# The feed-forward gradient at the normalised h1 as seven block products per pair of token tiles

## The chip, the cores and the metric

The kernel runs on one core of a Trainium2 chip. The metric is the device time of one execution in microseconds (us); lower is better. A core has TensorE (matrix products, PE in the profile), VectorE (DVE), ScalarE (ACT), GpSimd (POOL) and SyncE (SP). Each takes its own instructions in order; SP, POOL and ACT also issue DMAs. Products are accumulated in PSUM, here four tiles of two banks.

## The reference

Forward and backward of one block, S = 2048 tokens, width 640, 32 heads of 20, inner width 1728, bf16:

```
h   = x + ((phi(q) kv) / den) @ wo         q, k, v = LN(x) @ wqkv
      phi(t) = where(t > 0, t + 1, exp(t)) + 1e-6
      kv = sum_s phi(k) v    z = sum_s phi(k)    den = phi(q).z + 1e-6
out = h + (silu(LN(h) @ w_gate) * (LN(h) @ w_up)) @ w_down
```

Returned are out and the gradients of x, wqkv, wo, w_gate, w_up and w_down for a given gradient of out. What the change is about is the gradient at the normalised h1 (h before its layer norm is divided out): `dhn = [dg du] @ [w_gate w_up]^T`, a product of 2048 x 3456 by 3456 x 640, and what follows it: the layer norm's backward pass gives dh1, `dp = dh1 @ W2^T`, then dq, and dz, the gradient of z.

## The kernel before, in words

Tokens are 16 tiles of 128. The kernel first computes q and k, then the attention part (h1, its normalised form `hn`, its reciprocal deviation `rstd2`), then the FFN in four groups of inner columns (448, 448, 448, 384): gate and up products (L731, L736), elementwise work that makes the gradients `dd` (L764), and a `dw_group` for the weight gradients, whose products it already forms as seven block products (L646) beside plain ones (L806). `dd` is transposed by DMA and stored to `scr_dT` in HBM, 27 blocks of 128 rows for each token tile; the transposed weights stand in `wgT` (14 and 13 blocks of 128 x 640).

After the FFN comes the stage of this document (L846 to L921). In its loop over t:

- `load_cols` (L165) brings two token tiles of `scr_dT` (1728 KB) into one of four `strips` buffers.
- `mm_row` (L104) makes ps_dhn: 27 products for each of two column halves.
- `ln_bwd` (L141): ScalarE scales ps_dhn by rstd2 and sums it, VectorE multiplies with hn and sums, ScalarE makes `a`, VectorE adds twice; dh1 is transposed by DMA on SP's queue.
- Three tiles later (`LAG_C`): ps_dp from the transposed dh1; then VectorE: multiply by phi(q), sum per head, nS1 = -S1/den, zb x nS1, add, clamp phi(q) to phi'(q), two multiplications to dq. phi(q) is read from `scr_pq` by a POOL DMA; `pqs_tm` (phi(q)/den) is made from it (L886).
- `dz_add` (L833): two fp32 operations a tile, ten in the loop, six later under ps_dwqk.

`gt_part` (L858) sums over all tokens the products of dh1 and pqs_tm into five ps_gt; three of them start before the last ps_dp. Then ps_dwqk, ps_dkvt, ps_wk2, ps_dk and ps_dxn follow (L966 to L1077).

The framework gives buffers from pools (`big`: 5, `strips`: 4, `fpool`: 6, `psum`: 4) and makes an instruction wait for a free one. Within `tc.manual_schedule(engines=...)` the named engines keep the written order; elsewhere a planner orders instructions. In the stage before, SP and POOL keep the written order and TensorE, VectorE and ScalarE are planned.

Of the kernel before, what the change touches and what calls it, by code (L numbers as in the profile page):

```python
# [8 lines left out]
FP32 = mybir.dt.float32  # L9
# [6 lines left out]
P = 128  # L16
# [4 lines left out]
def kernel(  # L21
# [24 lines left out]
    MTA = 5  # L46
    assert (S, D, F) == (2048, 640, 1728)
# [35 lines left out]
    scr_pq, scr_pq_v = dram_tm("scr_pq", D)  # L83
    scr_h1, scr_h1_v = dram_tm("scr_h1", D)
# [527 lines left out]
    fpool = wB.enter_context(tc.tile_pool(name="fpool", bufs=6))  # L612
    zpad = wB.enter_context(tc.tile_pool(name="zpool", bufs=1)).tile([P, 4, 64], BF16, name="zpad")
    nc.gpsimd.memset(zpad[:], 0.0)

    with tc.manual_schedule(engines={EngineType.SP}):
# [6 lines left out]
        def hn_blk(m, k, u):  # L623
            i = 2 * m + u
            return hn[:, 8 * k:8 * k + 8, i * P:(i + 1) * P]

        def dw_group(g, w, m_s, dd, dw, dwd_part, dgu_part):
# [28 lines left out]
            S3 = [sums.tile([P, 8, P], BF16, name="S3", tag="S3", bufs=2) for _ in U]  # L656
            dw([dwd_part(0), dwd_part(1)], nc.vector.tensor_copy, first=True)
            for u in U:
                tt(S[u][:], hn_blk(1, 0, u), hn_blk(1, 1, u), ALU.add)
            for u in U:  # L660
                tt(S3[u][:], hn_blk(0, 0, u), hn_blk(1, 0, u))
            dw([dgu_part(4, 0), dgu_part(4, 1)], copy)
# [12 lines left out]
            store(ev, 0, 0)  # L675
            dw([dwd_part(4)], nc.vector.tensor_copy)
# [4 lines left out]
            tt(T3, B22, B12)  # L681
            dw([dwd_part(2), dwd_part(3)], nc.vector.tensor_copy)
# [4 lines left out]
            for u in U:  # L687
                prod(pa[u][:, 0, :w], S3[u], T3, False)
                copy(out=u3[:, u, :], in_=pa[u][:, 0, :w])
                tt(S[u][:], hn_blk(0, 1, u), S[u][:])  # L690
            ev = fw("dwev")
            tt(ev[:, :, :w], pc[:, :, :w], u3, ALU.add)
            store(ev, 1, 1)
            late = m_s[:, 12:16, :].rearrange("p (k u) n -> p k u n", k=2)
# [27 lines left out]
        for g in range(4):  # L722
# [53 lines left out]
            if g == 0:  # L776
                wdT = strips.tile([P, DT, 2 * GM], BF16, name="wdT", tag="S")
                load_wdT(wdT, 2)
            elif g == 1:
                wgT[0] = big.tile([P, 14, D], BF16, name="wgT", tag="B")  # L780
                for gg in range(2):
                    tr_wgT(gg)
                    load_wgu(gg + 2)
            elif g == 2:
                dm_t[3] = strips.tile([P, ST, GM], BF16, name="dm3", tag="S")
                act_load(dm_t[3][:, :, :GW[3]], scr_dm_v)
                wgT[1] = big.tile([P, 13, D], BF16, name="wgT", tag="B")
                tr_wgT(2)
                tr_wgT(3)
            else:  # L790
                for c in range(4):
                    pool_store(scr_m_v[:, c * 4:(c + 1) * 4, F:FT * P], m_s[:, c * 4:(c + 1) * 4, w - 64:w])
                pool_store(mat_v(scr_dwdT)[:, 0:4, F:FT * P], zpad[:])
                pool_store(mat_v(scr_dwdT)[:, 4, F:FT * P], zpad[:, 0, :])
                load_cols(0, act_load)

# [33 lines left out]
    mats = M.tile([P, 3 * DT * D], BF16, name="mats", tag="M")  # L830
    zacc = M.tile([P, D], FP32, name="zacc", tag="Z")

    def dz_add(t, tmp):  # L833
        prod = tmp if t else zacc[:]
        nc.vector.tensor_tensor(out=hb(prod), in0=hb(pqs_tm[:, t, :]), in1=bc(nS1[:, t, :]), op=ALU.mult)
        if t:
            nc.vector.tensor_tensor(out=zacc[:], in0=zacc[:], in1=tmp, op=ALU.add)
# [8 lines left out]
    with tc.manual_schedule(engines={EngineType.SP, EngineType.Pool}):  # L846
        W2T = mat(0, DT, D)
        nc.sync.dma_start(out=W2T[:], in_=mat_v(scr_W2T))
        woT = mat(DT * D, DT, D)
        dh1 = dh2  # L850
        pqs_tm = big.tile([P, ST, D], BF16, name="pqs_tm", tag="B")
        pqr = {}
        dwds = {}
        dh1Ts = {}

        gts = {}

        def gt_part(ps, i, t0, t1):  # L858
            for ci, (n0, n1) in enumerate(NCH):
                for t in range(t0, t1):  # L860
                    nc.tensor.matmul(ps[:, ci, :320], lhsT=dh1[:, t, i * P:(i + 1) * P], rhs=pqs_tm[:, t, n0:n1],  # L861
                                     start=(t == 0), stop=(t == ST - 1))

        ZL = 10
        ztmp = mats[:, 11 * D:13 * D].bitcast(FP32)
        dq = [strips.tile([P, 8, D], BF16, name="dq", tag="S") for _ in range(2)]
        for t in range(ST + LAG_C):
            if t < ST:
                if t % 2 == 0 and 2 < t + 2 < ST:
                    load_cols(t // 2 + 1)  # L870
                cols = colp[t // 2]
                if t >= 2:
                    dwds[t - 2] = wk("dwd", pool=1)
                    nc.sync.dma_start_transpose(out=dwds[t - 2][:].unsqueeze(1), in_=scr_dwdT[:, (t - 2) * P:(t - 1) * P])
                ps = mm("ps_dhn")
                mm_row(ps, lambda k: cols[:, t % 2, k, :],
                       lambda k, n0, n1: wgT[k // 14][:, k % 14, n0:n1], NKT)
                ln_bwd(ps, hn[:, t, :], rstd2[:, t:t + 1], dh2[:, t, :], dh1[:, t, :], 0)
                dh1T = wk("dh1T", pool=1)
                dh1Ts[t] = dh1T[:].rearrange("p (k c) -> p k c", c=P)  # L880
                last_dh1T = nc.sync.dma_start_transpose(out=dh1Ts[t], in_=dh1[:, t, :]).ins
            u = t - LAG_C + 1
            if u in range(ST):
                pqr[u] = wk("pqr", pool=1)
                nc.gpsimd.dma_start(out=pqr[u][:], in_=scr_pq_v[:, u, :])
                nc.vector.tensor_tensor(out=hb(pqs_tm[:, u, :]), in0=hb(pqr[u][:]), in1=bc(rall[:, u, :]), op=ALU.mult)  # L886
            if 0 <= t - LAG_C - 1 < ZL:
                dz_add(t - LAG_C - 1, ztmp)
            if 3 <= t < FT + 3:
                dwd = dwds.pop(t - 3)  # L890
                r0 = (t - 3) * P
                nc.gpsimd.dma_start(out=out_6[r0:min(r0 + P, F), :], in_=dwd[:min(P, F - r0), :])
            if t % 2 == 1 and t < 2 * DT:
                tr_piece(woT, A_wo, t // 2)
            if t % 4 == 2 and t >= 6:

                nc.gpsimd.dma_start(out=hn[:, t - 6:t - 2, :], in_=x_v[:, t - 6:t - 2, :])
            u = t - LAG_C
            if u < 0:
                continue  # L900
            if u == ST - 1:
                for i in range(3):
                    gts[i] = mm("ps_gt")
                    gt_part(gts[i], i, 0, ST - 3)
            pq = pqr.pop(u)
            dh1Tv = dh1Ts.pop(u)
            dp = wk("dp")
            ps = mm("ps_dp")
            mm_row(ps, lambda i: dh1Tv[:, i, :], lambda i, n0, n1: W2T[:, i, n0:n1], DT)
            nc.scalar.copy(out=half(dp[:]), in_=row(ps))  # L910
            pr = wk("pr")
            nc.vector.tensor_tensor(out=pr[:], in0=dp[:], in1=pq[:], op=ALU.mult)
            S1 = small.tile([P, H], FP32, name="S1", tag="S1", bufs=3)
            nc.vector.tensor_reduce(out=S1[:], in_=hb(pr[:]), axis=AX.X, op=ALU.add)
            nc.vector.scalar_tensor_tensor(out=nS1[:, u, :], in0=S1[:], scalar=-1.0, in1=rall[:, u, :],
                                           op0=ALU.mult, op1=ALU.mult)
            nc.vector.tensor_tensor(out=hb(pr[:]), in0=hb(zb[:]), in1=bc(nS1[:, u, :]), op=ALU.mult)
            nc.vector.tensor_tensor(out=dp[:], in0=dp[:], in1=pr[:], op=ALU.add)
            nc.vector.tensor_scalar(out=pq[:], in0=pq[:], scalar1=-1e-6, scalar2=1.0, op0=ALU.add, op1=ALU.min)
            nc.vector.tensor_tensor(out=dp[:], in0=dp[:], in1=pq[:], op=ALU.mult)  # L920
            nc.vector.tensor_tensor(out=hb(dq[u // 8][:, u % 8, :]), in0=hb(dp[:]), in1=bc(rall[:, u, :]), op=ALU.mult)  # L921

    with tc.manual_schedule(engines={EngineType.SP, EngineType.DVE}):
# [27 lines left out]
        for i in range(DT):  # L951
# [4 lines left out]
            else:  # L956
                gt_part(ps, i, ST - 3, ST)
            nc.scalar.copy(out=half(GT[:, i, :]), in_=row(ps))

# [44 lines left out]
        ztmp = ring[:, 0:2].rearrange("p a k c -> p (a k c)").bitcast(FP32)  # L1004
        for t in range(ZL, ZL + 2):
            dz_add(t, ztmp)
        dwqk(0, 0)
        kv_blocks(dKVT, "ps_dkvt", lambda i, a, b: woT[:, i, a:b], lambda i, a, b: GT[:, i, a:b])
        for t in range(ZL + 2, ST):
            dz_add(t, ztmp)  # L1010
        dzs = [wk("dzs"), wk("dzl")]
        nc.vector.tensor_copy(out=dzs[0][:], in_=zacc[:])
        nc.vector.tensor_tensor(out=dzs[1][:], in0=zacc[:], in1=dzs[0][:], op=ALU.subtract)
# [310 lines left out]
```

## Time and profile before

| | |
|---|---|
| time, median of 3 runs | 796.45 us (796.36 to 796.95) |
| the profiled execution | 796.25 us, span 794.5 us, granted clock 1.0 |
| TensorE busy | 790.2 us |
| VectorE busy | 566.9 us |
| first ps_dhn to end of ps_gt | 437.2 to 598.1 us |

A group's row gives line, engine, operation, output <- inputs, partitions x elements, count, then busy time and mean ns of one, then the idle time before it and who ended it. A matmul's duration overlaps that of the next, so its pace is read from the chain or the time line. Landing is the time from a DMA's issue to the arrival of its data.

### The profile page before, as it was taken

Reading aid. Unit: us, or ns where it says so; the run is one execution under the profiler, and the core shown is the slowest. Engines: PE = TensorE matmul, PEld = TensorE weight load, DVE = VectorE, ACT = ScalarE, POOL = GpSimd, SP = SyncE. Lnnn points to the kernel's source line nnn. Section 1 sums busy time; section 2 is a strip of 40 time slices with the busy share of each in tenths; the row PEclk is TensorE's granted clock in tenths of the full one; section 3 lists DMA queues with packets and bytes.
Section 4 is the critical chain, followed back from the end, with each engine's and each line's share of the span. In section 5 each row is a group of like instructions: output and inputs, shape, how many; then the busy total and the mean of one; then the engine's idle time right before and its main releaser. Section 6 shows DMA issues by size and latency. Waiting matters only on the chain.

```text
span 794.5 us, 13629 instructions
## 1 busy us (share of the span) xinstructions
PE 790.2 (99%) x5315; PEld 506.5 (64%) x5315; DVE 566.9 (71%) x1015; ACT 288.1 (36%) x414; POOL 172.7 (22%) x305
## 2 busy tenths in 40 slices
PE   9999999999999999999999999999999999999998
PEld 7776566555555555555666777777777777777665
DVE  7989988894497648845975259998897366635773
ACT  6962532760283045402831123223313133324010
POOL 4600047411201110012042102111221121113230
PEclk9999999999999999999999999999999999999999
DMA  9799999999679877892798657976598959999992
GB/s 259 161 241 305 198 225 254 257 264 234 176 160 236 211 175 191 217 246 68 147 216 217 247 152 193 211 197 168 127 238 177 177 135 155 189 223 261 208 259 83
DMA packets 286705, 160.11 MB, mean 202 GB/s; under 512 B 241564, under 2 KB 275485, under 8 KB 286640
## 3 DMA queue, kind: packets, MB, share of 16 engines
q1 hardware_dynamic: 268912, 99.56, 61.7%
q0 software_dynamic: 14832, 54.36, 22.4%
q10 hardware_dynamic: 2896, 5.33, 2.0%
q8 instruction: 41, 0.67, 0.4%
q14 instruction: 24, 0.20, 0.1%
HBM read 47.68 MB, written 53.66 MB: 128 GB/s over the span
## 4 chain that ended last, share of the span: by engine, by line
PE 97%; DMA 1%; DVE 1%; POOL 0%; issue 0%; SPq 0%; DVEq 0%
PE ps_dhn L108 15%; PE ps_dw L806 10%; PE ps_dxn L1069 8%; PE pu L736 7%; PE ps_wa L646 7%; PE pg L731 7%; PE ps_dwqk L986 5%; PE ps_dm L417 5%; PE ps_kq L305 4%; PE ps_oa L1139 4%; PE ps_wc L646 3%; PE ps_gt L861 3%; PE ps_dp L108 3%; PE ps_dk L108 3%; PE ps_y L508 3%; PE ps_a L571 3%
## 5 line engine op out<-in xcount | busy, mean ns | idle before, releaser
L108 PE MATMUL ps_dhn<-wgT,cols 128*128 128x320 bf16 x864 | 119.5, 299 | 0.0
L108 PEld LDWEIGHTS <-cols 128*128 128x128 bf16 x864 | 84.5, 98 | 32.9
L146 DVE CUSTOM_DVE_ANT_0 lb_a<-lb_dy,hn 128x640 bf16<-128x640 bf16 x32 | 26.4, 825 | 59.0 <-ACT lb_dy L144 59.0
L736 PE MATMUL pu<-wgu,hnT 128*128 128x448 bf16 (+1 forms) x320 | 63.6, 346 | 0.0
L731 PE MATMUL pg<-wgu,hnT 128*128 128x448 bf16 (+1 forms) x320 | 63.6, 346 | 0.0
L806 PE MATMUL ps_dw<-m_s,dh 128*128 128x448 bf16 (+1 forms) x320 | 60.4, 346 | 0.0
L1069 PEld LDWEIGHTS <-ring 128*128 128x128 bf16 x480 | 47.0, 98 | 18.2
L1069 PE MATMUL ps_dxn<-wqkvT,ring 128*128 128x320 bf16 x320 | 51.3, 299 | 0.0
L736 PEld LDWEIGHTS <-hnT 128*128 128x128 bf16 x320 | 31.3, 98 | 27.1
L806 PEld LDWEIGHTS <-dh 128*128 128x128 bf16 x320 | 31.3, 98 | 27.1
L731 PEld LDWEIGHTS <-hnT 128*128 128x128 bf16 x320 | 31.3, 98 | 27.0
L417 PEld LDWEIGHTS <-dh2T 128*128 128x128 bf16 x320 | 31.0, 98 | 25.1
L417 PE MATMUL ps_dm<-wdT,dh2T 128*128 128x448 bf16 (+1 forms) x240 | 46.5, 344 | 0.0
L144 ACT ACTIVATE lb_dy<-ps_dhn,rstd 128x640 bf16<-128x640 f32 x16 | 12.7, 794 | 91.5 <-PE ps_dhn L108 91.5
L305 PE MATMUL ps_kq<-wqk,xnT 128*128 128x320 bf16 x320 | 44.9, 299 | 0.3 <-DMA wqk<-in_A_wqkv_dram 0.2
L752 ACT ACTIVATE dd<-pg 128x896 bf16<-128x896 f32 (+1 forms) x32 | 28.5, 891 | 40.4 <-PE pg L731 38.0
L642 DVE TENSOR_TENSOR dd<-dd 128x3584 bf16<-128x3584 bf16 (+1 forms) x12 | 23.1, 1954 | 22.8 <-PE ps_wa L646 15.6
L305 PEld LDWEIGHTS <-xnT 128*128 128x128 bf16 x320 | 30.9, 98 | 12.7 <-issue 0.5
L646 PEld LDWEIGHTS <-S 128*128 128x128 bf16 x256 | 25.1, 98 | 21.7
L772 POOL DMA_DIRECT2D scr_m<-m_s x16 | 12.1, 758 | 122.6 <-DVE m_s L764 122.6
L986 PEld LDWEIGHTS <-hn 128*128 128x128 bf16 x320 | 31.0, 98 | 12.0
L150 ACT ACTIVATE lb_a<-hn,lb_k 128x640 bf16<-128x640 bf16 x32 | 29.5, 920 | 21.8 <-DVE lb_k L149 18.8
(210 smaller groups left out, 1527.1 us busy)
## 6 DMA issues: line engine op xcount, KB each, us to landing
scr_dT<-stg SPq DMA_DIRECT2D x48, 224.0 KB, 2.6
cols<-scr_dT POOLq DMA_DIRECT2D x6, 1728.0 KB, 8.4
scr_m<-m_s POOLq DMA_DIRECT2D x12, 448.0 KB, 4.6
cols<-scr_dT ACTq DMA_DIRECT2D x2, 1728.0 KB, 10.5
scr_dT<-stg SPq DMA_DIRECT2D x16, 192.0 KB, 2.3
scr_pq<-pqa SPq DMA_DIRECT2D x4, 640.0 KB, 4.6
scr_xnT<-xnT SPq DMA_DIRECT2D x4, 640.0 KB, 5.3
scr_pk<-pk SPq DMA_DIRECT2D x4, 640.0 KB, 4.6
```

The lines of the kernel that those rows point to most:

```text
L108: nc.tensor.matmul(ps[:, ci, :320], lhsT=lhs(k), rhs=rhs(k, *NCH[ci]), start=(start and k == 0), stop=(stop and k == n - 1))
L150: nc.scalar.activation(out=a[:], in_=xhat, func=ACT.Identity, scale=k[:, 1:2], bias=k[:, 0:1])
L305: nc.tensor.matmul(ps[:, ci, :320], lhsT=xnT[:, t, k, :], rhs=wqk[:, k, w0 + n0:w0 + n1], start=(k == 0), stop=(k == DT - 1))
L417: nc.tensor.matmul(ps[:, c, :w], lhsT=dh2T[:, kt, (t + c) * P:(t + c + 1) * P], rhs=wdT[:, kt, o:o + w], start=(kt == 0), stop=(kt == DT - 1))
L646: nc.tensor.matmul(out, lhsT=lhs[:, t, :], rhs=rhs[:, t, :], start=(first and t == 0), stop=(t == 7), skip_group_check=not first)
L731: nc.tensor.matmul(pg[:, c, :w], lhsT=hnT[:, kt, (t + c) * P:(t + c + 1) * P], rhs=wg[:, kt, 0:w], start=(kt == 0), stop=(kt == DT - 1))
L736: nc.tensor.matmul(pu[:, c, :w], lhsT=hnT[:, kt, (t + c) * P:(t + c + 1) * P], rhs=wg[:, kt, w:2 * w], start=(kt == 0), stop=(kt == DT - 1))
L752: sig = nc.scalar.activation(out=dg, in_=pg[:, :, :w], func=ACT.Sigmoid)
L806: nc.tensor.matmul(ps[:, c, :w], lhsT=lhs(t), rhs=rhs(t), start=(t == 0), stop=(t == ST - 1))
L986: nc.tensor.matmul(ps[:, ci, :320], lhsT=xn_r[:, t, i * P:(i + 1) * P], rhs=dq[t // 8][:, t % 8, n0:n1] if which == 0 else dk[:, t, n0:n1] ...
L1069: nc.tensor.matmul(ps[:, ci, :320], lhsT=lhs[:, i, :], rhs=rhs[:, i, n0:n1], start=(k == 0 and i == 0), stop=(k == 2 and i == DT - 1))
L1139: nc.tensor.matmul(out, lhsT=lhs[:, k, :], rhs=rhs[:, k, :], start=(start and k == 0), stop=(stop and k == HK - 1), skip_group_check=not s ...
```

## The change

**The product.** Two token tiles (rows) by two halves of the inner dimension (13 blocks each, one block left over) times two halves of it by two column halves: seven products of 13 matmuls in place of eight, with sums on both sides. Over A (left, from cols) and B (right, from wgT), S1 = A21+A22, S2 = S1-A11, S3 = A11-A21, S4 = A12-S2; T1 = B12-B11, T2 = B22-T1, T3 = B22-B12, T4 = B21-T2. In a step p TensorE does A11 B11, A12 B21, S4 B22 of the pair before, S1 T1, S2 T2, ps_dp of token f, S3 T3, ps_dp of token h, A22 T4. The left-over block adds four matmuls. Parts that a later product overwrites in the same bank are first copied to SBUF by ScalarE (s1, u2, u3), scaled by rstd2; VectorE's `comb` joins them.

**dz** becomes 32 matmuls of 32 stationary columns each, into four 32-row parts of one PSUM tile, masked and summed afterwards; `dz_add` is gone.

**phi(q)/den and phi'(q)/den** of tokens 0 to 14 are made by VectorE inside `dw_group` of the first three groups and stored to `scr_pqs` and `scr_w`; the stage reads them back. Token 15 is still made in the stage. The sums of wgT are made in the fourth `dw_group`.

**The order**: TensorE, VectorE, ScalarE, SP and POOL keep the written order in the stage. `pqs_tm` takes the `big` buffer that held T1, T2 and S1; the pq buffers and dy lie in spare blocks of wgT.

```diff
-    fpool = wB.enter_context(tc.tile_pool(name="fpool", bufs=6))
+    fpool = wB.enter_context(tc.tile_pool(name="fpool", bufs=7))
...
+        def pq_norm(ts):
+            for t in ts:
+                pq, out = pq_in.pop(t), flat("pqs")
+                nc.vector.tensor_tensor(out=hb(out), in0=hb(pq), in1=bc(rall[:, t, :]), op=ALU.mult)
+                pool_store(scr_pqs_v[:, t, :], out)
+                nc.vector.tensor_scalar(out=pq, in0=pq, scalar1=-1e-6, scalar2=1.0, op0=ALU.add, op1=ALU.min)
+                nc.vector.tensor_tensor(out=hb(pq), in0=hb(pq), in1=bc(rall[:, t, :]), op=ALU.mult)
+                pool_store(scr_w_v[:, t, :], pq)
...
+            if g < 3:
+                pq_load(range(5 * g, 5 * g + 3))
             dw([dwd_part(0), dwd_part(1)], nc.vector.tensor_copy, first=True)
...
+            if g < 3:
+                pq_norm(range(5 * g, 5 * g + 3))
+            else:
+                wg_tsum(1)
...
+            if g < 3:
+                pq_norm(range(5 * g + 3, 5 * g + 5))
+            else:
+                wg_tsum(3, 6, HKG)
+                col_sum(0, 1)
+                col_sum(0, 3)
...
-        for t in range(ST + LAG_C):
...
-            if 0 <= t - LAG_C - 1 < ZL:
-                dz_add(t - LAG_C - 1, ztmp)
...
+        def prod(out, p, lhs, rhs, first=False, left=None):
+            for k in range(HKG):
+                nc.tensor.matmul(out, lhsT=lhs[:, k, :], rhs=rhs[:, k, :], start=(first and k == 0),
+                                 stop=(k == HKG - 1), skip_group_check=not first)
...
+        for p in range(NPR):
+            t1, t2 = 2 * p + 1, 2 * p
+            q1, q2 = t1 - 2, t2 - 2
+            f, h = 2 * p - 3, 2 * p - 2
+            if p > 0:
+                ln_a(q2, dy2)
+            if p != 1:
+                p1(p)
+            Y[p] = mm("ps_dhc")
+            A, C, Dd = X[p][:, 0, :320], Y[p][:, 0, :320], Y[p][:, 1, :320]
+            prod(Dd, p, col_blk(p, 0, 1), B21, first=True, left=(0, BL[:, 0:320]))
+            col_sum(p, 2)
+            if p > 0:
+                ln_b(q2)
+                if h - 2 in dps:
+                    dp_a(h - 2)
+                ln_c(q2, dy2)
+                if h - 2 in dps:
+                    dp_b(h - 2)
...
+            col_sum(p, 4)
+            if p > 0:
+                p3(p - 1)
+                c12(p - 1)
+                ln_a(q1, dy1)
+            if p + 2 < NPR:
+                load_cols(p + 2)
+            for x in (p5, p6) if f >= 0 else (p6, p5):
+                x(p)
+            if p > 0:
+                ln_b(q1)
...
+            if f >= 0:
+                load_q(f)
+                dp_mm(f)
+            prod(A, p, col_blk(p, 1, 0), T3, left=(1, BL[:, 320:D]))
+            scaled(u3, A, p, 1)
+            if p == NPR - 1:
+                pqs_tm = big.tile([P, ST, D], BF16, name="pqs_tm", tag="B")
...
+            if p > 0:
+                ln_c(q1, dy1)
+            if h >= 0:
+                load_q(h)
+                dp_mm(h)
+            comb(dy1[:, 0:320], Dd, p, 0, s1)
+            if f >= 0:
+                dp_a(f)
+            comb(dy2[:, 320:D], C, p, 1, u3)
+            if f >= 0:
+                dp_b(f)
+            if p + 1 < NPR:
+                col_sum(p + 1, 1)
+                col_sum(p + 1, 3)
+            if p == 0:
+                p1(1)
+            prod(A, p, col_blk(p, 1, 1), T4, left=(1, T5))
+            scaled(dy2[:, 0:320], A, p, 1)
...
+        for i in range(3):
+            gts[i] = mm("ps_gt")
+            gt_part(gts[i], i, 0, ST - 4)
...
+        for t in (ST - 2, ST - 1):
+            dp_mm(t)
+        for t in (ST - 2, ST - 1):
+            dp_a(t)
+            dp_b(t)
...
+        ps_dz = mm("ps_dz")
+        for ci, (n0, n1) in enumerate(NCH):
+            for t in range(ST):
+                c = 32 * (t % 4)
+                nc.tensor.matmul(ps_dz[c:c + 32, ci, :320], lhsT=nS1[:, t, :], rhs=pqs_tm[:, t, n0:n1],
+                                 start=(t < 4), stop=(t >= ST - 4))
```

The helpers: `ln_a` is ScalarE's sum over dy, VectorE's product with hn and its sum, and the small scaling `k`; `ln_b` is ScalarE's `a`; `ln_c` is the two additions to dh1 and its transposing DMA. `dp_mm` is ps_dp and its copy, `dp_a` the multiply by phi(q), the sum per head and nS1, `dp_b` zb x nS1, the addition and the multiply by phi'(q)/den (for token 15 also pqs_tm, the clamp and one multiply more). `load_q` brings phi(q) and phi'(q)/den of a token by POOL. `c12` is the `comb` of the upper right block.

## The prediction

> **What bounds the kernel now.** I read the page's header and engine totals first, then the groups by form, then the chain of waits, then the time line and windows of the stage that the change rewrites.
>
> ```profile
> span 794.5 us, 13629 instructions
> ...
> PE 790.2 (99%) x5315; PEld 506.5 (64%) x5315; DVE 566.9 (71%) x1015; ACT 288.1 (36%) x414; POOL 172.7 (22%) x305
> ...
> L108 PE MATMUL ps_dhn<-wgT,cols 128*128 128x320 bf16 x864 | 119.5, 299 | 0.0
> ```
>
> TensorE never rests; the 864 products of ps_dhn are its largest group. The chain that ended last, in order of time, gives their pace:
>
> ```profile
> 476.62 7.33 PE ps_dhn L108 x54
> 485.32 7.33 PE ps_dhn L108 x54
> ```
>
> 54 products in 7.33 us are 135.8 ns each (the 299 ns of the group overlap). A token tile takes 8.69 us: 54 products and the 10 of ps_dp. The windows (us, then busy time of PE, PEld, DVE, ACT, POOL, clock, DMA share, GB/s) show who is next:
>
> ```profile
> 467.00:571.00 104.00, 104.00 (x767) 74.91 (x766) 93.39 (x187) 29.67 (x49) 18.88 (x32) 1.00 0.73 187
> ```
>
> VectorE is busy for 93.4 of 104 us. So this stage has two engines near their limit, and any saving on TensorE larger than some 10% hands the stage to VectorE. Its prices are in the time line, as distances between starts:
>
> ```profile
> 486.08 0.49 DVE L912 TENSOR_TENSOR pr<-dp,pqr 128x640 bf16<-128x640 bf16 x1
> ...
> 486.61 0.82 DVE L914 TENSOR_REDUCE S<-pr 128x32 f32<-128x640 bf16 x1
> ...
> 487.34 0.48 DVE L151 TENSOR_TENSOR lb_a<-lb_a,lb_dy 128x640 bf16<-128x640 bf16 x1
> 487.74 0.18 DVE L915 SCALAR_TENSOR_TENSOR nS<-S,rall 128x32 bf16<-128x32 f32 x1
> 487.84 0.32 DVE L919 TENSOR_SCALAR pqr<-pqr 128x640 bf16<-128x640 bf16 x1
> ```
>
> An operation that needs the one before it starts after that one's full duration plus 0.04 (0.53 after the 0.49 multiply); an independent one starts 0.08 to 0.09 before its end (0.40, 0.73, 0.10). The planner's order here interleaves two tokens; the new order is written out and mostly puts dependent operations next to each other.
>
> [...] 1024 elements take 682 ns and 3584 take 2020, 0.523 ns each beyond a fixed part. [...] the pqr load issued right behind a column load landed after 10.6 us, the others after a median of 2.7.
>
> The tile views of pqr and of cols say:
>
> ```profile
> DMA to landing us min/median/max: 2.5/2.7/10.6
> ```
>
> ```profile
> DMA to landing us min/median/max: 8.1/8.6/11.4
> ```
>
> **TensorE, part by part.** A pair of tiles had 108 products of ps_dhn; seven products of 13 and four left-over ones are 95. Eight pairs save 104, at 135.8 ns 14.1 us. A step with its two ps_dp is 115 products, 15.62 us, against 17.38. dz adds 32 products: 4.35 us one after another, [...]
>
> **VectorE, a pair in the new order.** Two ln_a without their waits, 0.75+0.11+0.10 each: 1.92. Four column sums of 1664 elements: 0.682+640x0.523 ns = 1.02, next start 0.09 sooner, 0.93 each: 3.72. Two dp_a, 0.53+0.86+0.10: 2.98. Two ln_c, 0.53+0.40: 1.86. Two dp_b, 0.86+0.53+0.40: 3.58 ([...] the 0.82 multiply by rall, the clamp and the 0.82 that made pqs have gone to the FFN). Three combinations from PSUM: the nearest row is 491 ns for 128x320, plus 65 for the scalar column (882 against 817 ns in L1041): 0.59+0.47+0.47 = 1.53. Sum 15.59. And one idle time that nothing fills: after ln_a of q1 VectorE's next instruction is ln_c of q1, which needs ScalarE's ln_b: 0.17+0.03+0.92+0.04, less the 0.10 counted, about 1.06, and 0.2 because the copy to u2 stands ahead of ln_b on ScalarE. So 16.85 us for a pair, 1.2 more than TensorE and 0.5 less than before. **VectorE sets the pace.** It holds TensorE at the fifth product, S3 x T3: that overwrites the bank which ScalarE copies to u2, and this copy is queued behind ln_a's sum over dy1, which waits for VectorE's c12. From the start of VectorE's step c12 begins at 7.03, ends at 7.6, and u2 is free at about 9.15.
>
> **The stage, added up.** Zero is the first ps_dhn (437.2). Steps 0 and 1 have 94 and 92 products and little VectorE work: TensorE alone sets them, 25.26 us. Step 2 of VectorE starts in effect at 26.35 (its S2 waits for the first product to end at 27.3). Five periods later, at 110.6, step 7 starts; S3 x T3 of it at 119.75. From there TensorE has 14+10+14+14+10+72+20+88 = 242 products, 32.86 us: ps_gt would end at 152.6. Before, 1184 products took 160.8.
>
> To this come four costs:
> - The pq load of token f is now issued behind load_cols, which waits for the pair before to leave its strip (S4 x B22). In step 2 that is at 31.0; cols lands 8.4 later, pq about 0.9 after it, 40.3, where dp_a wants it at 37.8: 2.5 late. Later steps give some of it back. Bounds 0 and 4; I take 2.0.
> - Three ps_gt tiles hold three of the four PSUM tiles, so the last ps_dp waits for the copy of the one before: 0.26+0.69, 0.95.
> - pqs_tm, 2.6 MB on SP's queue, is issued in step 7 ahead of dh1T of token 13, which TensorE wants some 5 us later (landings of dh1T so far 2.6 to 7.4): 0 to 3, I take 1.0.
> - dz 1.5.
>
> Sum 158.05, 2.8 us less than before.
>
> **What I cost at nothing.** In the FFN 15 tiles get three operations each (about 1.85 us a tile, 9.3 a group), the last group the sums of wgT (three of 4160 elements, 2.3 each) and two column sums. They lie beside TensorE's weight-gradient products, where VectorE was busy for 23.2 of 42.4 us in the first group and 21.5 of 36.4 in the last. Their DMAs are 2.4 MB a group, 57 GB/s on top of 227; POOL issues them, and its queue there only stores. The exposed place is T1 in the first group, which waits for the transposes out of dd until 188.8 and ends 2.2 us before its product: 0 to 2.5 us there, taken as 0. dz_add was on VectorE under the products of ps_dwqk; its removal frees nothing on the path. The mask for dz is made by POOL under ps_gt. wgT now also holds the pq buffers, so wqkvT can load only from about 578 (576.8 before); its first six pieces took 19.7 us and are wanted at about 605. xnT_r starts near 586, needs 12.9, is wanted near 612.
>
> The profiled execution took 796.25 us for its span of 794.5, 0.2 under the median of 796.45; the 2.8 come off either. Forecast 793.7.
>
> **Rivals.**
> - *TensorE keeps the pace* (0.18). For it: issue distances are from one interleaved stretch, and a pair is only 1.2 us over. Then 14.1 less 1.5 less 0.95 are saved: 784.8. Against it: four column sums alone are 3.7 us, and the idle time at ln_b is in the written order.
> - *The last tile of pqs stops TensorE, slower* (0.20). The operation making pqs of token 15 stands inside dp_b of 15, behind dp_a and dp_b of 14; counted from step 7 it ends at 36.8. TensorE is through the last ps_dp at 31.2 and meets that tile 3 products later. If it takes the fourth ps_gt and tiles 12 to 14 first (48 products, 6.5 us) it is covered, as in my sum; if the order stays as written, it stands for 5.2 us: 798.9. It decides from 2.8+1.6 = 4.4 us.
> - *The pq transfers set the pace* (0.12). The loop S3 x T3, S4 x B22, cols, pq, dp_a, next step is 35 us for two steps at a landing of 9.3 us; if pq lands 12.7 after the column issue it is 19.2 a step, and four such steps cost some 7 us over my sum: 800 to 803.
>
> **How the numbers follow.** My own case has 0.50, with 790.5 to 797.5 from its unknowns. A measurement of this kernel can tell about 0.2% (1.6 us) from no change. Faster: 0.18, and 0.32 of my case; same: 0.15 of my case and 0.02 of the second rival; slower: 0.03 of my case, 0.18 and 0.12. The range 787.5 to 802 leaves out most of the first rival and the far end of the third.
>
> **What would show it.** ps_dhn and ps_dhc together 760 products; a step of the new stage 16.5 to 17.5 us in the chain; VectorE above 90% in the windows there, TensorE about 93% with one gap a step in front of S3 x T3, released by ScalarE's copy to u2. FFN groups as long as before (42.4, 42.3, 42.3, 36.4). A gap before ps_gt released by pqs_tm is the second rival; dp_a waiting for the pq DMA the third. I am wrong if steps last 15.7, or if the FFN or the products after ps_gt show gaps.

## The result, and the profile after

The changed kernel takes 819.12 us (median of 4; 816.20 to 828.58) against 796.4 us: 1.0272 times, 95% interval 1.0236 to 1.0308. The forecast was a gain, 793.7 (787.5 to 802); it became a loss of 2.7%. The profiled execution is the longest, 828.58 us, so a second one of the same kernel (817.72 us) stands beside it; where executions scatter, the ratios count the undisturbed ones only, the medians all.

| us | before | after | after, second profile | forecast |
|---|---|---|---|---|
| up to the first product on h1 | 437.1 | 440.0 | 438.2 | 437.2 |
| from there to the first ps_dwqk | 160.8 | 176.4 | 179.0 | 158.05 |
| from there to the end | 196.6 | 210.4 | 198.8 | 196.6 |
| span | 794.5 | 826.9 | 816.0 | |

The times of the first row come from the tile views of ps_dhn, those of ps_dwqk from its own. Most of the loss, 15.6 to 18.2 us, is in the rewritten stage; 1 to 3 us come from the FFN and 2 to 14 from behind the stage. The page after, in the order of the one before:

```profile
span 826.9 us, 13706 instructions
...
PE 789.8 (96%) x5243; PEld 499.5 (60%) x5243; DVE 600.1 (73%) x1048; ACT 301.4 (36%) x446; POOL 209.8 (25%) x370
...
PE 64%; DVE 13%; DMA 10%; issue 8%; SPq 2%; ACT 1%; POOL 1%; DVEq 0%; POOLq 0%; ACTq 0%
```

72 matmuls fewer, the same busy time, and a chain of which a third (36%; 3% before) is no longer TensorE. What TensorE waited for (engine, tile, line, releaser: us in total, times, longest):

```profile
PE ps_dwv L130 <- DMA mats<-scr_Yt: 8.2, 2, 5.8
PE ps_dhn L937 <- ACT dq L1008: 6.9, 3, 3.6
PE ps_gt L912 <- DVE pqs_tm L998: 6.7, 1, 6.7
PE ps_dp L111 <- DMA dh1T<-dh: 5.7, 2, 4.4
PE ps_wc L689 <- DVE dd L685: 1.5, 2, 1.2
PE pu L799 <- DMA wgu<-in_B_w_up_dram: 1.3, 1, 1.3
```

Before, the stage had none. The second row is S3 x T3 waiting for ScalarE's copy to u2, as the forecast had it, but for 3.6 us at once. TensorE's time line of one such stop and of the end of the stage:

```profile
495.63 3.25 PE L937 MATMUL ps_dhn<-wgT,cols 128*128 128x320 bf16 x13 [3.62 <-ACT dq L1008]
498.68 0.47 PE L941 MATMUL ps_dhn<-wgT,cols 128*128 128x320 bf16 x1
498.94 1.78 PE L111 MATMUL ps_dp<-mats,dh1T 128*128 128x320 bf16 x10
500.56 1.93 PE L937 MATMUL ps_dhn<-mats,cols 128*128 128x320 bf16 x13
...
578.19 2.85 PE L111 MATMUL ps_dp<-mats,dh1T 128*128 128x320 bf16 x10 [4.40 <-DMA dh1T<-dh]
580.83 10.22 PE L912 MATMUL ps_gt<-pqs_tm,dh 128*128 128x320 bf16 x72
590.89 1.52 PE L111 MATMUL ps_dp<-mats,dh1T 128*128 128x320 bf16 x10
...
604.38 10.95 PE L912 MATMUL ps_gt<-pqs_tm,dh 128*128 128x320 bf16 x64 [6.69 <-DVE pqs_tm L998]
615.26 1.27 PE L1177 MATMUL ps_dz<-pqs_tm,nS 128*32 128x320 bf16 x32
```

Read the distances between starts, against 135.8 ns a product. Behind the stop of 3.62 us, 24 products take 4.93 us (495.63 to 500.56), not 3.26; behind that of 4.40 us, 82 take 12.70, not 11.14; behind that of 6.69 us, 64 take 10.88, not 8.69. These stops are paid twice: first the wait, then 1.6 to 2.2 us of slow products. The four stops of over 2 us in this stage (3.62, 2.43, 4.40, 6.69) cost 1.7, 1.7, 1.6 and 2.2 more, 7.1 in all.

The windows of these four stretches (start:end and length, busy time of PE, PEld, DVE, ACT and POOL, granted clock of TensorE, DMA share, GB/s) show what made the products slow:

```profile
495.63:500.56 4.93, 4.93 (x24) 2.95 (x24) 3.67 (x8) 1.87 (x3) 1.09 (x2) 0.65 0.82 183
532.68:537.61 4.93, 4.93 (x25) 2.84 (x25) 4.04 (x8) 1.86 (x3) 0.97 (x2) 0.65 0.94 233
578.19:590.89 12.70, 12.70 (x83) 8.61 (x83) 7.50 (x15) 2.34 (x4) 3.72 (x7) 0.87 0.28 66
604.38:615.26 10.88, 10.88 (x64) 7.02 (x63) 3.91 (x10) 2.77 (x4) 3.09 (x4) 0.80 1.08 210
```

A mean clock of 0.65 over 4.93 us loses 0.35 x 4.93 = 1.7 us; the same working gives 1.7, 1.7 and 2.2 for the others, which is what the products lost. Before, the clock was 1.00 throughout the stage (437.2 to 598.1 us).

The first stop starts with VectorE. Its time line, and GpSimd's, which issues the load it waits for:

```profile
480.90 0.49 DVE L981 TENSOR_TENSOR pr<-dp,wgT 128x640 bf16<-128x640 bf16 x1 [3.34 <-DMA wgT<-scr_pq]
```

```profile
467.26 1.13 POOL L1100 DMA_DIRECT2D out_dram<-dwd  x2 [8.35 <-DMA dwd<-scr_dwdT]
471.34 0.71 POOL L163 DMA_DIRECT2D cols<-scr_dT  x1 [2.95 <-PE ps_dhc L941]
472.05 0.57 POOL L966 DMA_DIRECT2D wgT<-scr_pq  x1
```

phi(q) of token f is issued 0.7 us behind 1.7 MB of columns and lands 8.8 us later. VectorE stands 3.34 us, and everything in its written order is late by that: c12, ln_a(q1)'s sum on ScalarE, the copy to u2 behind it, and 14.7 us later S3 x T3.

At the end of the stage VectorE makes phi(q)/den of token 15 (L998), with work of the next stage woven in:

```profile
594.61 0.43 DVE L981 TENSOR_TENSOR pr<-dp,wgT 128x640 bf16<-128x640 bf16 x1
594.96 1.06 DVE L1222 TENSOR_SCALAR hn<-hn,mv,rstd 128x640 bf16<-128x640 bf16 x1
...
597.11 0.43 DVE L1222 TENSOR_SCALAR hn<-hn,mv,rstd 128x640 bf16<-128x640 bf16 x1
...
603.51 0.81 DVE L998 TENSOR_TENSOR pqs_tm<-wgT,rall 128x640 bf16<-128x640 bf16 x1
```

Nine operations of L1222, which belong to the next stage, stand between the first multiply of token 14 and this one; the eight of 0.43 advance the queue by 0.36 each, the first by 0.98, 3.9 us together.

### The profile page after: what moved, and what is told of

It reads as the page before. It is cut to its first block, busy times and chain, and to the rows that moved or that the text cites. A ratio compares the mean times of both kernels' runs of the same rounds, so it can differ in the third digit from the quotient of the medians.

```text
span 826.9 us, 13706 instructions
## 1 busy us (share of the span) xinstructions
PE 789.8 (96%) x5243; PEld 499.5 (60%) x5243; DVE 600.1 (73%) x1048; ACT 301.4 (36%) x446; POOL 209.8 (25%) x370
## 4 chain that ended last, share of the span: by engine, by line
PE 64%; DVE 13%; DMA 10%; issue 8%; SPq 2%; ACT 1%; POOL 1%; DVEq 0%; POOLq 0%; ACTq 0%
PE ps_dxn L1286 8%; PE ps_dw L873 6%; PE ps_dm L420 5%; PE ps_wa L689 5%; PE ps_dwqk L1206 5%; PE pg L794 4%; PE ps_kq L308 4%; PE pu L799 3%; PE ps_oa L1356 3%; PE ps_y L511 3%; PE ps_a L574 3%; PE ps_wc L689 3%; PE ps_dk L111 2%; DMA wgT<-scr_pq 2%; PE ps_dhn L937 2%
## 5 line engine op out<-in xcount | busy, mean ns | idle before, releaser
L937 PEld LDWEIGHTS <-cols 128*128 128x128 bf16 x624 | 61.6, 99 | 32.7 <-issue 7.5
L420 PE MATMUL ps_dm<-wdT,dh2T 128*128 128x448 bf16 (+1 forms) x240 | 46.5, 344 | 0.0
L937 PE MATMUL ps_dhn<-wgT,cols 128*128 128x320 bf16 x208 | 33.0, 312 | 6.9 <-ACT dq L1008 6.9
L149 DVE CUSTOM_DVE_ANT_0 lb_a<-lb_dy,hn 128x640 bf16<-128x640 bf16 x16 | 13.2, 825 | 30.8 <-ACT lb_dy L147 30.8
L141 POOL TENSOR_SCALAR lnv<-mv 128x1 f32<-128x1 f32 x32 | 11.9, 373 | 89.1 <-DVE mv L137 73.2
L111 PE MATMUL ps_dp<-mats,dh1T 128*128 128x320 bf16 x160 | 26.7, 317 | 5.7 <-DMA dh1T<-dh 5.7
L912 PE MATMUL ps_gt<-pqs_tm,dh 128*128 128x320 bf16 x160 | 24.9, 319 | 7.1 <-DVE pqs_tm L998 6.7
```

The costliest lines, as they stand in the source:

```text
L111: nc.tensor.matmul(ps[:, ci, :320], lhsT=lhs(k), rhs=rhs(k, *NCH[ci]), start=(start and k == 0), stop=(stop and k == n - 1))
L420: nc.tensor.matmul(ps[:, c, :w], lhsT=dh2T[:, kt, (t + c) * P:(t + c + 1) * P], rhs=wdT[:, kt, o:o + w], start=(kt == 0), stop=(kt == DT - 1))
L937: nc.tensor.matmul(out, lhsT=lhs[:, k, :], rhs=rhs[:, k, :], start=(first and k == 0), stop=(k == HKG - 1), skip_group_check=not first)
```

## The experiments

The stage is read in three parts: the loop, from the product A22 x T4 of step 2 to that of step 7 (five steps; forecast 5 x 16.85 + 2.0 = 86.3); the end, from there to the first ps_dwqk (forecast 33.0); and the rest.

| kernel | median us | ratio, 95% interval | loop | end | rest |
|---|---|---|---|---|---|
| before | 796.4 | | | | 196.6 |
| after | 819.12 | 1.0272 (1.0236–1.0308) | 90.8 | 46.7 | 210.4 |
| after, again | 817.72 | one execution | 92.1 | 46.5 | 198.8 |
| dh1T(13) first | 817.88 | 1.0268 (1.0229–1.0307) | 94.0 | 45.3 | 197.0 |
| token 15 early | 818.04 | 1.0258 (1.0233–1.0282) | 94.7 | 38.0 | 204.3 |
| phi(q) ahead | 814.30 | 1.0198 (1.0157–1.0240) | 86.8 | 47.3 | 198.0 |
| these three | 806.49 | 1.0124 (1.0069–1.0178) | 84.5 | 36.1 | 205.1 |
| these, wqkvT early | 805.67 | 1.0089 (1.0055–1.0124) | 84.3 | 37.0 | 198.2 |
| token 15 early, wqkvT early | 816.46 | 1.0250 (1.0203–1.0296) | 95.1 | 41.6 | 196.9 |

### The changed kernel again

> The changed kernel once more, for a second profile. If its loss is fixed in the program, FFN, stage and tail are longer than before by the same amounts as in the first profile (3.0, 15.5 and 14 us). If the tail's part comes from how DMAs happen to meet, that part differs (the three shorter runs leave 4 to 8 us for it) and FFN and stage stay within about 1 us.

817.72 us. The same three stops in the stage (dq 7.7 us in all, pqs_tm 6.2, dh1T 5.5) and only 1.6 us at ps_dwv, which had 8.2. So the stops of the stage belong to the kernel; those behind it vary between executions.

### dh1T(13) ahead of pqs_tm

```diff
+            if p > 0:
+                ln_c(q1, dy1)
             if p == NPR - 1:
                 pqs_tm = big.tile([P, ST, D], BF16, name="pqs_tm", tag="B")
...
-            if p > 0:
-                ln_c(q1, dy1)
```

> The pqs_tm load is issued after dh1T of token 13 in place of ahead of it; nothing else. Theory late transfer: dh1T of 13 landed 9.2 us after its issue because 2.6 MB stood ahead of it; TensorE's wait of 4.4 us there, the wait of VectorE for ScalarE's sum (5.6) and most of the wait for pqs_tm of 15 (6.7) are one chain, so the kernel gets 8 to 11 us faster. Rival written order: the wait for pqs_tm of 15 comes from its place behind dp_a and dp_b of 14 alone; then only the 4.4 and the slow products behind it go, 4 to 6 us, and the 6.7 stay. If neither, under 1 us, because pqs_tm now lands late and ps_gt waits for it.

No gain, for the last of the three reasons that were expected. The wait for dh1T(13) is gone from the end of the stage; ps_gt waits 3.0 us for pqs_tm's own DMA instead, and 6.1 for token 15 as before. Putting the one transfer first made the other late, and token 15 stops TensorE whichever it is.

### phi(q)/den of token 15 early

```diff
             else:
                 pq = pq_b[t % 2]
-                nc.vector.tensor_tensor(out=hb(pqs_tm[:, t, :]), in0=hb(pq), ...)
...
         dp_b(ST - 3)
+        nc.vector.tensor_tensor(out=hb(pqs_tm[:, ST - 1, :]), in0=hb(pq_b[(ST - 1) % 2]), ...)
```

> The operation that makes pqs_tm of token 15 moves ahead of dp_a of 14 on VectorE; nothing else. Rival written order: TensorE's wait of 6.7 us before ps_gt goes, kernel 5 to 7 us faster. Theory late transfer: the wait goes too, but VectorE is as late as before and the next thing it owes, dq of 15 and the xn rows for ps_dwqk, stops TensorE some 12 us later, so 2 to 5 us faster.

The end of the stage is 8.5 to 8.7 us shorter (38.0 against 46.5 and 46.7), and the time does not move. In this profile 2.6 to 3.9 us of it went in a longer loop (94.7). TensorE's time line of this kernel shows what took most of the rest:

```profile
598.56 11.30 PE L912 MATMUL ps_gt<-pqs_tm,dh 128*128 128x320 bf16 x82
609.79 1.27 PE L1177 MATMUL ps_dz<-pqs_tm,nS 128*32 128x320 bf16 x32
...
644.83 0.84 PE L1286 MATMUL ps_dxn<-wvk,ring 128*128 128x320 bf16 x5 [2.30 <-DMA wvk<-wvk]
647.72 2.84 PE L1286 MATMUL ps_dxn<-wqkvT,ring 128*128 128x320 bf16 x10 [2.05 <-DMA ring<-dk]
```

And SyncE's queue of the same kernel:

```profile
590.15 1.20 SPq L963 DMA_TRANSPOSE dh1T<-dh  x1
599.12 8.15 SPq L1147 DMA_TRANSPOSE wqkvT<-in_A_wqkv_dram  x6
607.32 28.30 SPq L903 DMA_TRANSPOSE wqkvT<-in_A_wqkv_dram  x10
635.72 1.22 SPq L1192 DMA_TRANSPOSE ring<-scr_pk  x1
...
638.43 6.54 SPq L1199 DMA_TRANSPOSE wvk<-wvk  x5
```

wqkvT takes the buffer of wgT, and that buffer now also holds phi(q) of token 14, which is read (dp_a) 9 us after the last dh1T. The 16 transposes are issued from 599.1 (before: from 576.8) to 635.6, and ring and wvk queue behind them. In this profile the gain became waits of 4.4 us one stage later.

### phi(q) ahead of the next pair's columns

```diff
+            if f >= 0:
+                load_q(f)
             if p + 2 < NPR:
                 load_cols(p + 2)
...
             if f >= 0:
-                load_q(f)
                 dp_mm(f)
```

> On POOL's queue the phi(q) and phi'(q)/den loads of token f go ahead of the column load in place of behind it; nothing else. Theory transfers: VectorE's waits for phi(q) in the loop (3.3 us in step 2, some 3 in step 4) go, and with them TensorE's gaps of 3.6 and 2.4 us and the slow products behind them: 4 to 8 us faster. Rival VectorE's work: the steps last what VectorE needs, 16.9 us, with or without these waits: under 2 us faster.

The largest gain of a single edit, ratio 1.0198, though its interval still touches that of the changed kernel. (Its profiled execution, 824.04 us, stood 8.0 us at ScalarE's first copy, ahead of the loop.) phi(q) lands after a median of 4.6 us in place of 6.8, VectorE no longer waits for it, and the loop takes 86.8 us against 90.8 to 95.1 in the kernels without the edit; the forecast was 86.3. The forecast's pace was there, behind this transfer.

### All three, and wqkvT's buffer freed early

> Edit: the three edits of the runs before together (the load of pqs_tm issued behind the transpose of dh1T(13); phi(q)/den of token 15 made before its gradient arrives; each pair's phi(q) and phi'(q)/den loads issued ahead of the next pair's columns). Theory A, 'three late transfers in the stage, and a fourth that takes over behind it': the stage, from the first product on h1 to the first ps_dwqk, falls from 177 us to about 166 (pq 4, token 15 6.7, dh1T 0 to 1), but wqkvT's transposes still begin only when the last phi(q) buffer inside wgT has been read, so ps_dxn waits 4 to 8 us behind it for wvk or ring; time 811 (807 to 815). Rival B, 'the gains add and nothing takes them back': 798 + no wait at ps_dxn, time 805 to 807. Rival C, 'VectorE's own work sets the stage and the waits only show where': stage stays above 172, time 814 or more.

806.49 us, and a stage of 159.6 us: what single edits hid adds up when they are made together. The time is rival B's (805 to 807), but the waits at ps_dxn, which B excluded, are there as in theory A, smaller than it expected, 2.1 and 2.4 us:

```profile
631.01 0.84 PE L1287 MATMUL ps_dxn<-wvk,ring 128*128 128x320 bf16 x5 [2.06 <-DMA wvk<-wvk]
634.23 2.85 PE L1287 MATMUL ps_dxn<-wqkvT,ring 128*128 128x320 bf16 x10 [2.39 <-DMA ring<-dk]
```

The next kernel moves what keeps wgT occupied into the unused end of the second dq strip:

```diff
-                dq.append(strips.tile([P, 8, D], BF16, name="dq", tag="S"))
+                dqs1 = strips.tile([P, 14 * 4 * P], BF16, name="dq", tag="S")
+                dq.append(dqs1[:, :8 * D].rearrange("p (t d) -> p t d", t=8))
+                late[12], late[14], late["dy1"] = (dqs1[:, (8 + i) * D:(9 + i) * D] for i in range(3))
```

> Edit: the run with the three edits, and besides phi(q) of tokens 12 and 14 and dy of token 15 put in the unused end of the second dq strip in place of wgT, so that the buffer that wqkvT takes is free as soon as TensorE has done with wgT. Theory A: wqkvT's transposes begin within 2 us of the last dh1T, 6 to 8 us earlier than in the run with three edits; the waits at ps_dxn go; stage 160 to 166; time about 801 (796 to 806). Rival B (what takes the gain back is not where wqkvT's transposes start): the same time as with three edits, within 2 us. Rival C (VectorE's work sets the stage): 812 or more.

Its SyncE queue and TensorE's time line:

```profile
575.70 8.94 SPq L1158 DMA_TRANSPOSE wqkvT<-in_A_wqkv_dram  x6
584.69 14.22 SPq L903 DMA_TRANSPOSE wqkvT<-in_A_wqkv_dram  x10
```

```profile
570.53 0.70 PE L912 MATMUL ps_gt<-pqs_tm,dh 128*128 128x320 bf16 x4 [2.48 <-DMA pqs_tm<-scr_pqs]
572.71 10.53 PE L912 MATMUL ps_gt<-pqs_tm,dh 128*128 128x320 bf16 x64 [1.48 <-DMA pqs_tm<-scr_pqs]
...
586.73 11.30 PE L912 MATMUL ps_gt<-pqs_tm,dh 128*128 128x320 bf16 x82
```

The transposes are issued from 575.7 to 598.9 (before: 576.8 to 611.1); no product of ps_dxn waits, and the rest is 198.2 us against 205.1. The profiled execution took 799.14 us, the median 805.67: the ratio fell to 1.0089, its interval overlaps that of the three edits. By the medians it is rival B, the same time within 2 us. So the trace shows that the waits are gone, and the times do not show a gain from it. What still stops TensorE at the end of the stage is pqs_tm's DMA, 4.0 us, which cannot start before T1, T2 and S1 leave its buffer.

> Edit: of the changed kernel two things alone: phi(q)/den of token 15 made before its gradient arrives, and phi(q) of tokens 12 and 14 and dy of token 15 out of wgT, so that wqkvT's buffer comes free earlier. The first alone took 7 us out of the stage and gave 818.0. Theory A (the late wqkvT transposes gave it back): no wait at ps_dxn, time 811 to 813. Rival (given back elsewhere, whatever the transposes do): 816 to 819.

816.46 us: by time, the rival. By the profile there is no wait at ps_dxn and the rest is 196.9; but in that execution the end is 41.6, with a 7.6 us wait for dh1T(13), and the first product on h1 comes at 447.3, 10 us later than before. A gain of 6 us can't be read from the time of a kernel whose other stops vary by as much. Inconclusive.

### VectorE's load or the transfers

The column sums are left out from the second pair on, in the kernel with phi(q) ahead:

```diff
+            if p == 0:
-            col_sum(p, 2)
+                col_sum(p, 2)
...
-            if p + 1 < NPR:
-                col_sum(p + 1, 1)
-                col_sum(p + 1, 3)
```

> Edit: the run with phi(q) ahead of the columns, with the column sums left out from the second pair on (28 sums of 1.02 us; the products then read columns as loaded, so this leaves out part of the computation). It takes 4.1 us per pair from VectorE and nothing from TensorE or the queues. Theory A (with phi(q) in time, VectorE's 16.9 us per pair set the pace, 17.2 measured): steps 2 to 7 now take TensorE's 15.6 us each, 78 us from the start of step 2 to that of step 7 against 85.9 with the sums; no wait of S3xT3 for ScalarE's copy. Rival (the transfers of dh1T, columns and phi(q) or ScalarE's queue set the pace): 83 us or more, and the waits for ScalarE's copy or dh1T stay.

Against theory A: the loop took 88.2 us, not 78, though 4.1 us of VectorE's work per pair were gone (the expectation counted from the starts of steps, 85.9 with the sums; by the measure of the table it was 86.8). Some steps took the 15.62 us of TensorE alone, two took 18.6 and 22.7. The longer is on VectorE's time line, and its cause on GpSimd's:

```profile
538.74 0.49 DVE L981 TENSOR_TENSOR pr<-dp,wgT 128x640 bf16<-128x640 bf16 x1 [7.83 <-DMA wgT<-scr_pq]
```

```profile
516.63 0.55 POOL L1100 DMA_DIRECT2D out_dram<-dwd  x1 [11.18 <-DMA dwd<-scr_dwdT]
517.36 0.55 POOL L1100 DMA_DIRECT2D out_dram<-dwd  x1 [0.18 <-issue]
517.91 0.76 POOL L1104 DMA_DIRECT2D hn<-in_A_x_dram  x1
...
519.73 0.71 POOL L163 DMA_DIRECT2D cols<-scr_dT  x1
520.43 0.57 POOL L966 DMA_DIRECT2D wgT<-scr_pq  x1
```

GpSimd's queue stood for 11.2 us behind a store that waits for the transpose of dwd; then it issued x, columns and phi(q) of the next token at once, and that phi(q) arrived 18.3 us later. In this profile, with VectorE faster, the transfers set the stage at once. In the two mended kernels VectorE's pace is seen. On its time line with all four edits its one regular idle time, the wait for ScalarE in front of ln_c(q1), comes every 16.9 to 17.0 us:

```profile
508.82 0.49 DVE L959 TENSOR_TENSOR lb_a<-lb_a,wgT 128x640 bf16<-128x640 bf16 x1 [1.04 <-ACT lb_a L955]
...
525.74 0.49 DVE L959 TENSOR_TENSOR lb_a<-lb_a,wgT 128x640 bf16<-128x640 bf16 x1 [1.04 <-ACT lb_a L955]
```

In between VectorE stands nowhere. TensorE's own steps there last 15.6 to 18.3 us: in the loop it waits 2.0 us for the copy to u2 and 3.4 at ps_dp, whose weights are dh1T. So the transfers are close behind VectorE.

### The FFN part and dz, each alone in the kernel before

> Edit: the kernel before, with only the part of the change in the FFN: phi(q) of 15 tokens loaded, normalised with its derivative by three VectorE operations a token, both stored to scratch; nothing reads the stores, the rest is as before. Theory A (the FFN part costs by the transfers it puts among the transposes): first product of ps_dhn 1 to 6 us later than 437.1 and times that scatter by several us, median 799 (797 to 803). Rival (my forecast's price: nothing, VectorE and queues have room): 796.5 within 0.5 us, no scatter.

800.51 us (median of 22), ratio 1.0048 (1.0026 to 1.0070), executions from 797.1 to 812.2. The waits of TensorE in its profile, which the kernel before does not have:

```profile
PE ps_wc L668 <- DVE dd L664: 1.6, 1, 1.6
PE pu L766 <- DMA wgu<-in_B_w_up_dram: 0.8, 1, 0.8
```

The changed kernel has the same two waits, but there ps_wc waits in the first FFN group, here in the second. Here the sum that it waits for stands on VectorE behind nine operations on phi(q), which had waited 5.3 us for its load. With the loads and stores alone and no VectorE operation:

> Edit: the kernel before with the transfers of the change's FFN part alone: phi(q) of 15 tokens loaded and stored twice to scratch at the same places, without the three VectorE operations a token. Theory A (the transfers cost, by standing among those of dd and wgu): a ratio near the 1.0048 of the whole FFN part, 1.003 to 1.006, with the same scatter. Rival (the VectorE operations ahead of the T1 to T3 sums cost): within 0.1 % of before.

800.23 us, 1.0046 (1.0025 to 1.0067), executions from 796.3 to 808.8. Within the intervals the loads and stores cost as much as the whole FFN part; VectorE's operations are not needed for it. Whether it is their traffic or the buffers that they hold was not separated.

> Edit: the kernel before, with only dz by column tiles: the 31 VectorE additions for dz left out, 32 products of 32 columns and one masked copy in their place. Theory A (TensorE has no wait in this stage before, so its 32 products of 1.2 us in all come on top): 797.6 (797.0 to 798.0). Rival (VectorE's dz additions held TensorE back somewhere): 796 or less. Rival (the stop at the column tiles' accumulation or the mask made by GpSimd stalls the start of ps_dwqk): 799 or more.

798.53 us, 1.0038 (1.0018 to 1.0058), 0.9 us above theory A's 797.6. In its profile the 32 products take 1.20 us, one after the other at the end of ps_gt, and nothing stalls:

```profile
598.69 1.27 PE L967 MATMUL ps_dz<-pqs_tm,nS 128*32 128x320 bf16 x32
599.89 1.40 PE L996 MATMUL ps_dwqk<-dq,hn 128*128 128x320 bf16 x9
```

The first product on h1 is also 0.7 us later there, behind a wait of 0.8 us at ps_kq that the edit doesn't touch. Eleven of the 18 executions, the profiled one among them, took 797.6 to 798.9 us; the other seven, 802.7 to 804.8, had a mean granted clock of 0.996 to 0.998 in place of 1.0. Of the 39 of the kernel before beside them four took over 800. So 1.2 us are the products; the rest of the 0.38% comes with the seven, of which no profile was kept.

### What remains

> Edit: the run with phi(q) ahead, token 15 early, dh1T(13) first and wqkvT's buffer freed early, without the FFN part: no loads, products and stores of phi(q)/den and phi'(q)/den there; the stage on h1 loads phi(q) and phi(k) in their places, same sizes (this leaves out part of the computation). Theory A (what remains of the loss with all four mends is mostly the FFN part, 3 to 4 us): time 798 to 802, 4 us under the run with the FFN part, and runs of it above 803 become few. Rival (the stage's transfers still cost the rest): 803 or more.

Against theory A: 806.86 us (ratio 1.0125, 1.0103 to 1.0147), no better than with the FFN part. Its first product on h1 comes at 437.5, near the 437.1 of before, so that in this profile the FFN's cost is gone; but the stage takes 163.5 and the rest 203.8, with 3.2 us at ps_dwv for scr_Yt and slow products behind it (granted clock 0.98 on the mean from 700 to 804 us). Three runs asked whether this stop, moved, is what remains:

```diff
-                if p != 2:
+                if p != 1:
                     f, i = small_q.pop(0)
                     f(i)
```

> Edit: the run with phi(q) ahead, token 15 early, dh1T(13) first and wqkvT's buffer freed early, and in the last stage the first product of dwv one pair of tokens later, so that it stands 7 us further behind the transposes of scr_Yt that it reads. Theory A (what is left beside the 3.8 us of the FFN part is TensorE stopped at dwv by transposes that come late in some executions, 0.9 to 3.5 us seen, and the slow products after it): median 801 (799 to 803), no wait at ps_dwv. Rival (the last stage is late for other reasons, its transposes of m or its stores): 803 to 806 as without the edit, and the wait moves to ps_oa.

> Edit: the changed kernel, with the first product of dwv one pair of tokens later in the last stage. Theory A: the wait for scr_Yt's transposes, 8.2 us in the profile and 1.6 in the other, goes; median 815 to 817 against 818, fewer executions above 820. Rival (the wait moves on to the next reader of the same queue): no change, 817 to 820.

> Edit: the kernel before, with the first product of dwv one pair of tokens later in the last stage. Its profile shows no wait there. Theory A: 796.5, the same within 0.3, perhaps fewer executions near 800. Rival (the place of that product matters of itself): over 0.5 us either way.

The mended kernel: 804.69 us, 1.0058 (1.0031 to 1.0085), which overlaps 1.0089 without the edit; by time it is the rival's 803 to 806, but there is no wait at ps_oa, and its profile still has 1.9 us at ps_dwv, for scr_Yt. The changed kernel: 825.83 us, 1.0314 (1.0254 to 1.0374), no gain; a wait of 1.8 us at ps_dwv stays and its stage takes 183.0. The kernel before: 796.69, 1.0009 (0.9995 to 1.0023), the same. So the stop at dwv is not settled as what remains: TensorE's wait for scr_Yt differs between the profiles with the new stage, from none to 8.2 us, and the edit did not end it. No version that was run beats the kernel before.

## Why the prediction was wrong

**Right: prices and pace.** TensorE's step is 15.62 us wherever nothing holds it, steps 0 and 1 took 25.26 us (440.05 to 465.31), dz 1.2 us for 1.5 (the 1.5 was my own figure, with no run of such products behind it). VectorE's 16.85 us per pair is the loop of the mended kernels: 84.3 / 5 = 16.9. S3 x T3 is held by the copy to u2, as described, but in the mended loop that is only 2.0 us of 5.4; the rest is at ps_dp. With the late transfers mended the stage is 159.6 (three edits) and 160.7 us (four), 1.6 and 2.7 over my 158.05, and in it 3.4 and 4.0 us of pqs_tm's DMA.

**Wrong, the first of the four added costs: phi(q) behind load_cols, 2.0 us with bounds 0 and 4.** Taking it away alone brought the loop to 86.8 us, with the other edits to 84.3 to 84.5, against 90.8 to 95.1. The landing was right: forecast 9.3 from the column issue, measured 9.5. (That phi(q) comes late behind the columns on GpSimd's queue is read from its landings in the changed kernel: 8.8 us there, 2.5 at the least.) "Later steps give some of it back" was wrong: with VectorE as the pace-maker nothing gives it back, the stop recurs about every second step, and behind those of 3.62 and 2.43 us TensorE was slow (1.7 us lost each). My third rival (0.12; +7 us over my sum) was this mechanism.

**Wrong, the second rival kept apart: token 15.** I had it at 5.2 us and let 48 products of other tiles cover it. TensorE did take 24 (6, 3 and 15, from 592.25 to 597.7) and then stood for 6.7 us. From the last ps_dp, the sum counted 5.6 us of VectorE's work; it took 9.8, 3.9 of them the nine normalisations of the next stage. VectorE's order is written out in both stages, but the two orders are woven together where they meet; I had not asked what may stand between.

**Wrong, dh1T(13) behind pqs_tm, 1.0 us with bounds 0 and 3.** It landed after 9.2 us, and TensorE stood 4.4. Behind it ScalarE's copy of dp(13) stands ahead of ln_a(15)'s sum, so that VectorE waited 5.6 us too. But mending it alone gave nothing: pqs_tm was then late.

Together: by S3 x T3 of step 7 the loop was at 126.5 us for a forecast of 121.75, and from there the stage took 49.9 for 36.3. The 13.6 are 3.4 for dh1T, 6.1 for token 15 (with 0.4 at the copy of dp, less the 0.95 I had for that), 3.8 for slow products, less 0.3 on dz; 0.6 are spread.

**Wrong, the cost at nothing: the FFN.** I had put 0 to 2.5 us at T1 of the first group, taken as 0; alone it costs 3.8 us. The place was right in the changed kernel (the first ps_wc, waiting for dd), but it was not the only one: wgu's loads are late too. And the delay ahead of the stage varies: 1.1 and 3.0 us in the two profiles of the changed kernel, 10 us in two of its variants (the first product on h1 at 447.3 with token 15 and wqkvT early, at 447.6 in the mended kernel with dwv later).

**Wrong, the cost at nothing: wqkvT.** "From about 578" took the end of wgT's matrices as the release. The buffer is released by its last reader, phi(q) of token 14, and the transposes start at 595 to 599. That took nothing in the kernel as it is, where the stage is late anyway; it took 4.4 and 4.5 us in waits from the two versions that mend the end of the stage without mending this, and made their rest 6 to 7 us longer.

**Never in the sum: the slow products.** 7.1 us in the profiled stage. The granted clock there was 0.50 in four stretches, 496.05 to 499.46 us, 533.60 to 537.01, 577.97 to 581.38 and 601.87 to 608.69, and 1.00 between them. The parts of these behind the stops, 3.41, 3.41, 3.2 and 4.3 us, lose half their length at that clock: the 1.7, 1.7, 1.6 and 2.2 us of above. A stop of 2.43 us had such a stretch behind it here, and after one of 2.15 us in the kernel with phi(q) ahead 10 products took 2.2 us, not 1.36. A stop of 3.33 us in the run without the FFN part left the clock at 1.00 (10 products in 1.37 us), so that its length alone does not decide; what does, no run showed.

**Open.** It is open where the mended kernel's last 0.3 to 1.2% go: the FFN part's 0.48% and the 0.38% of dz would fill it, but the run without the FFN part does not fall by that. The profile of 799.14 us shows little of it, because it is one of the shortest executions: this one and that of 798.94 us had a mean granted clock of 0.998, the four at 805.3 to 807.0 one of 0.991 to 0.996. In the profile of the changed kernel each of the five stretches at clock 0.50 ahead of the last product begins in a stop of TensorE or within 0.9 us of its end. So the longer executions probably stood more often; where, no profile shows.

## What to carry to other kernels

A kernel whose TensorE waits nowhere may have its transfers in an order that just fits, as here: before a rewrite is priced by engine work, list for each buffer its last reader and for each queue what now stands ahead of what, to the end of the next stage. Where several stops lie one behind another, mending one may show little or nothing in the time; read each part of the stage in the profile, and mend them together before judging the idea. Here the idea itself was worth nothing: 14 us less of TensorE became a stage of 159.6 to 160.7 us at VectorE's pace against 160.8, and the transfers and dz added outside it cost more than that.

## What the runs showed of the hardware that was not expected

- Some stops of TensorE cost more than their length: 24 products took 4.93 us in place of 3.26 after 3.6 us, at a mean granted clock of 0.65; ten took 2.64 in place of 1.36 after 4.4 us, 64 took 10.88 in place of 8.69 after 6.7. The shortest single stop with slow products behind it was 2.15 us, in the kernel with phi(q) ahead. After 0.8 and 1.3 us in the changed kernel (14 products in 1.90 us, 23 in 3.14), and once after 3.3, in the run without the FFN part, none was seen.
- Column tiles: 32 products of 32 columns in 1.20 us, 37.5 ns each against 135.8, 3.6 times, with no visible stop on entering or leaving them in the run of dz alone.
- In one kernel (column sums left out), the shortest landing of a 160 KB load on GpSimd's queue was 2.4 us and the longest 18.3, behind 2.7 MB issued in the 2.5 us before it.
